# ScalarE issues the key loads in the middle of a group's second slot instead of at the end of its first

## The chip, the cores and the metric

The kernel runs on one core of one Trainium2 chip. The metric is the time of one execution on the device, in microseconds (us); lower is better. Engines are named as in the profile: PE is TensorE (PEld its weight loads), DVE is VectorE, ACT is ScalarE, POOL is GpSimd and SP is SyncE, which here only issues DMA transfers. A DMA instruction of SP or ACT is shown as SPq or ACTq: its duration is the time that the issuing queue spends on it, and its landing is when the data is there.

## The reference

Keys and values are one tensor, pooled 4 x 4 and projected; 4 batches of 12,288 tokens attend to 768 keys each, and every token then goes through a feed-forward layer of width 1,024 with a SoLU activation and a layer norm.

```python
kv_pool = kv.reshape(B, H // r, r, W // r, r, C).mean(axis=(2, 4))
k = v = kv_pool.reshape(B, -1, C) @ w_sr
s = scale * (q @ k.transpose(0, 2, 1))
a = np.exp(s - s.max(-1, keepdims=True))
x = (a / (a.sum(-1, keepdims=True) + 1e-09)) @ v
h = x @ w_in
e = np.exp(h - np.max(h, axis=-1, keepdims=True))
solu = h * (e / (np.sum(e, axis=-1, keepdims=True) + 1e-09))
ln = (solu - mean(solu)) / np.sqrt(var(solu) + 1e-06) * g_ln
out = ln @ w_out
```

## The kernel before

The 49,152 tokens are 384 tiles of 128 tokens. A **slot** is one step of the main loop, with a piece of work of several tiles at different stages; four slots make a **group** (512 tokens). The order of every instruction is written out by hand, so each engine's queue is that order with the other engines' instructions taken out. In slot `t` the kernel

- turns the scores of tile `t` into weights: `nm` (DVE, L611), the exponential `s` (ACT, L612), the high half of `phl` (ACT, L614), its low half (DVE, L622), and a DMA transpose of `phl` to `pT` (SP, L625);
- works on the hidden layer of tiles `t-11` and `t-10`: `u` (DVE, L741), the halves of `uhl` (POOL, L758 and L765), a DMA transpose of `uhl` to `uT` (SP, L780), the square `junk` of `u` for the variance (ACT, L806), the exponential `e` (ACT, L727);
- multiplies `uT` of tile `t-13` by the output weights (PE, L831; 24 weight loads and matmuls for a tile).

Once per group SP also loads the next queries (`qf`, 256 KB, L531), at the end of the group's last slot, and writes the finished rows (`out`, L863), and ACT scales the attended values to `xh` (L657), at the end of the first slot.

**Key loads.** While batch `b-1` is worked on, the 16 pieces of the next batch's keys come in as loads of 384 KB (`kv_load`, L230), which POOL adds up (`kv_add`, L241). `kv_plan` says in which slot each load and each add stands. The first 22 loads are issued by SP at the start; the other 42 are issued by ACT, one in every group or every second group. `kv_plan` rounds a piece's slot down to the first slot of its group, and the loop issues it as the last thing of that slot.

**Semaphores of transfers.** Each DMA instruction is given one of eight semaphores in turn (`DMAHW0` to `DMAHW7`), and does not start before the transfer that had this semaphore last has landed. Where a load stands in the program so decides on which earlier transfer it waits, and which later one waits on it.

Of the kernel before, what the change touches and what calls it, by code (L numbers as in the profile page):

```python
# [31 lines left out]
GT = 4  # L32
# [29 lines left out]
FIT_AT = 302  # L62

SOON = {0: (), 1: (8, 8), 2: (8, 8), 3: (27, 33), 4: (39, 45), 5: (51, 54)}
LATE = {6: (12, 16, 18), 7: (16, 20, 22)}


@with_exitstack
def kernel(
# [82 lines left out]
    def kv_alloc(b):  # L152
        for n, w, dt, bufs in (
            ("kT", NK, F32, 1),
            ("ksq", NK, BF16, 1),
            ("kss", 2, F32, 4),
            ("vf", NK, F32, 1),
        ):
            state[n, b] = bat.tile([P, w], dt, tag=n, name=f"{n}_{b}", bufs=bufs)
        for n, w in (("knm", 3), ("sv", 2), ("bb", 5), ("kq", 3), ("dg", P)):  # L160
            state[n, b] = (
                state[n, 0]
                if 0 < b < B
                else bat.tile([P, w], F32, tag=n, name=f"{n}_{b}", bufs=1)
            )
        for n, dt, bufs in (
            (("kwh", F32R, 1), ("kwl", F32R, 1))
            if b == 0 or b >= B
            else (("kh", F16, 2), ("kl", F16, 2))
        ):  # L170
            state[n, b] = bat.tile([P, NK], dt, tag=n, name=f"{n}_{b}", bufs=bufs)
        vhl = dmt.tile([P, 2 * NKC, P], F16, tag="vhl", name=f"vhl_{b}")
        state["vhl", b] = vhl
        state["vh", b], state["vl", b] = vhl[:, :NKC, :], vhl[:, NKC:, :]
# [327 lines left out]
    def kv_plan(b):  # L502


        for pos in range(RR):


            if b == 1 and pos in SOON:
                for half, slot in enumerate(SOON[pos]):
                    yield slot, [partial(kv_add, b, half, pos)]  # L510
                continue
            slot = 6 * pos - (28 if b == 1 else 30)
            load, *adds = (slot // GT * GT, slot + 3, slot + 5)
            if b == 1 and pos in LATE:
                load, *adds = LATE[pos]
            yield load, [partial(kv_load, b, pos)]
            if pos:
                for half, add in enumerate(adds):
                    yield add, [partial(kv_add, b, half, pos)]
        for slot, half, *fs in key_steps(b):  # L520
            yield slot, [partial(f, b, half) for f in fs]
# [18 lines left out]
    def wide(g):  # L540
        return g < GPB or g >= NG

    def q_scale(g):
        if wide(g) or NG <= g:
            return
        qf = state["qf", g // QL][:, (g % QL) * 512 : (g % QL + 1) * 512]
        nc.gpsimd.tensor_scalar(
            qf, qf, state["kq", g // GPB][:, 1:2], 1.0, op0=ALU.mult, op1=ALU.mult
        )
# [17 lines left out]
    def q_low(g):  # L567
        if NG <= g < NG + GPB:
            return
        qf = state["qf", g // QL][:, (g % QL) * 512 : (g % QL + 1) * 512]  # L570
        qh, ql = state["q", g]
        if wide(g):
            nc.gpsimd.tensor_tensor(
                in_tiles(ql), by_tile(qf), in_tiles(qh.bitcast(F32)), op=ALU.subtract
            )
        else:
            nc.gpsimd.tensor_tensor(ql, qf, qh, op=ALU.subtract)
# [52 lines left out]
    def values(g, qtr, part):  # L630
        share = {0: [0, 9, 9, 0], 1: [0, 6, 6, 6]}.get(
            g, [4, 5, 5, 4] if wide(g + 2) else [5, 5, 4, 4]
        )
        s0 = sum(share[:qtr])
        s1 = s0 + share[qtr]
        if s0 == s1:
            return
        cut = s0 + (s0 > 0 and (qtr > 1 or wide(g + 2)))
        s0, s1 = ((s0, cut), (cut, s1))[part]
        b = g * GT // TPB  # L640
        if s0 == 0 and s1:
            state["xa", g] = ps_x.tile([P, 512], F32, tag="x", name=f"xa_{g}")
        if s0 == s1:
            return
        xa, pT = state["xa", g], state["pT", g]
        vh, vl = state["vh", b], state["vl", b]
        seq = [(a, c, v) for c in range(NKC) for (a, v) in ((0, vh), (1, vh), (0, vl))]
        for n in range(s0, s1):
            a, c, v = seq[n]
            nc.tensor.matmul(  # L650
                xa, v[:, c, :], pT[:, :, a * NKC + c, :], start=n == 0, stop=n == len(seq) - 1
            )
# [386 lines left out]
    def key_steps(b):  # L1039
        steps = [  # L1040
            (70, 0, kv_kp, kv_ko), (71, 1, kv_kp, kv_ko), (74, 2, kv_kp, kv_ko),
            (72, 0, kv_sq), (75, 1, kv_sq),
            (77, 0, kv_kh), (79, 1, kv_kh),
            (78, 0, kv_kl), (80, 1, kv_kl),
        ]
        if b < B - 1:
            return steps + [
                (82, 0, kv_vp, kv_vo), (83, 1, kv_vp, kv_vo), (86, 2, kv_vp, kv_vo),
                (84, 0, kv_v_high), (85, 0, kv_v_low), (87, 1, kv_v_high), (88, 1, kv_v_low),
            ]  # L1050
        return steps + [
            (82, 0, kv_v_scale), (84, 1, kv_v_scale),
            (83, 0, kv_vt_high), (86, 1, kv_vt_high),
            (86, 0, kv_vt_low), (88, 1, kv_vt_low),
            (90, 0, kv_v_turn),
        ]
# [3 lines left out]
    def at(t, fn, *args):  # L1060
        if 0 <= t < NT:
            fn(t, *args)

    def at_last(t, fn, *args):

        if 0 <= t < NT and t % GT == GT - 1:
            fn(t // GT, *args)

    def at_soon(t, fn):

        at_last(t, fn) if t >= GT else fn(0) if t == GT - 2 else None

    plan = {}
    for b in range(1, B):
        for k, fs in kv_plan(b):
            plan.setdefault((b - 1) * TPB + k, []).append(fs)
# [4 lines left out]
    for slot in range(NT):  # L1081
        i = slot - LH
        av, qtr = divmod(slot - LAV - GT + 1, GT)
        tb, ti = divmod(slot, TPB)
        if ti == 12 and tb + 1 < B:
            kv_alloc(tb + 1)
        qs = GT if slot < 2 * GT else 2 * GT + 1 if slot < 3 * GT else 3 * GT + QSP
        todo = plan.pop(slot, [])
        at(slot, scores_exp)
        for f in held:  # L1090
            f()
        held = []
        if slot <= LH:
            at(slot - 1, scores_split)
        at(i - 1, hidden_u)
        at_last(slot - XSP - 1, values_split)
        if slot < 9:
            for f in fill.pop(slot, []):
                f()
        if 0 <= av < NG:  # L1100
            values(av, qtr, 0)
        if slot != 8:
            at(slot + 2 if slot < 8 else slot + 1, scores_pe)
        at_soon(slot - NORM, values_norm)
        at_last(slot - FSC, final_scale)
        at(i - 1, hidden_high)
        at(i - 1, hidden_low)
        at_last(slot - FSC, final_root)
        if slot < NT and 0 < qs < slot and (slot - 1 - qs) % GT == 0:
            q_low(slot // GT + 1)  # L1110
        if slot < NT and 0 < qs <= slot + 1 and (slot + 1 - qs) % GT == 0:
            q_scale((slot + 1) // GT + 1)
        if slot < NT - 1:
            at(i - 1, hidden_var)
        at(i, hidden_max)
        at(i, hidden_exp)
        if slot == NT - 1:
            hidden_var(i - 1)
        for f in fill.get(slot, []):
            f()  # L1120
        pairs = [st for st in todo if len(st) > 1 and st[0].func is not kv_add]
        for st in pairs:
            st[0]()
        if 0 <= av < NG:
            values(av, qtr, 1)
        for st in pairs:
            held += st[1:]
        if slot >= LH:
            at(slot, scores_split)
        at_soon(slot - NORM, values_recip)  # L1130
        at_soon(slot - NORM, values_recip_u)
        at(i + 1, hidden_pe)
        if slot < NT - 1:
            at(slot - LO, final_pe)
        at(i - 1, hidden_turn)
        if slot % GT == GT - 1:
            q_load(slot // GT + 3)
        at_last(slot - LO - 1, final_out)
        at_last(slot - XSP, values_out)
        for st in todo:  # L1140
            if st[0].func is kv_add:
                for f in st:
                    f()
            elif len(st) == 1:
                st[0]()
        if slot < NT and 0 < qs <= slot and (slot - qs) % GT == 0:
            q_split(slot // GT + 1)
# [182 lines left out]
```

## Time and profile before

| | before |
|---|---|
| time, median of 3 runs | 1836.55 us (1835.77 to 1844.36) |
| the profiled execution's own time | 1841.4 us |
| its span, first to last instruction | 1839.5 us |
| PE busy | 1818.2 us, 99% of the span |
| DVE, ACT, POOL busy | 1768.4, 1749.2, 1665.6 us (96%, 95%, 91%) |
| mean granted TensorE clock | 0.999 |
| key loads issued by ACT | 42 of 384 KB, 4.4 us to landing (median) |

A busy share is an average over the span. An engine that is busy for 99% of it leaves little for the others to win or lose by, so what counts here is the idle time of PE, and what ended it.

### The profile page before, as it was taken

What the parts mean: (1) busy time and instruction counts of PE and PEld (TensorE: products, weight loads), DVE (VectorE), ACT (ScalarE), POOL (GpSimd) and SP (SyncE); (2) the same over time, 40 slices, a digit from 0 to 9 for tenths busy, and PEclk for the clock granted to TensorE, in tenths of its full rate; (3) what the DMA queues carried; (4) which work ended last, traced back from release to release, by engine and by line L of the source; (5) the groups of instructions that cost most, each with busy time, mean ns of one, the idle gap of its engine ahead of it and who ended that gap; (6) DMA issues with size and microseconds to landing.
All of it is one profiled execution on the core that took longest, in us unless ns stands there. A gap on an engine that the chain in (4) does not pass through costs nothing.

```text
span 1839.5 us, 42799 instructions
## 1 busy us (share of the span) xinstructions
PE 1818.2 (99%) x15747; PEld 1216.9 (66%) x15747; DVE 1768.4 (96%) x2635; ACT 1749.2 (95%) x3129; POOL 1665.6 (91%) x1466
## 2 busy tenths in 40 slices
PE   8999999999999999999999999999999999999998
PEld 5577777777666666566666666666666666666666
DVE  6999999999999999999999999999999999999997
ACT  5999999999999999899999999999999999999997
POOL 5899999899999999889999999998988988888887
PEclk9999999999999999999999999999999999999999
DMA  8999999999999999999999999999999999999998
GB/s 301 202 243 241 237 242 242 237 230 231 250 230 250 250 233 234 225 245 235 235 244 249 236 243 248 244 233 221 233 240 231 222 230 229 235 227 236 223 226 170
DMA packets 1440026, 432.79 MB, mean 235 GB/s; under 512 B 1404608, under 2 KB 1408832, under 8 KB 1439552
## 3 DMA queue, kind: packets, MB, share of 16 engines
q1 hardware_dynamic: 1433616, 413.45, 111.3%
q10 hardware_dynamic: 6192, 16.52, 3.5%
q8 instruction: 126, 2.06, 0.5%
q14 instruction: 92, 0.75, 0.1%
HBM read 52.50 MB, written 25.17 MB: 42 GB/s over the span
## 4 chain that ended last, share of the span: by engine, by line
PE 82%; ACT 8%; DVE 3%; DMA 2%; issue 2%; POOL 2%; SPq 0%; DVEq 0%; POOLq 0%; ACTq 0%
PE o L831 24%; PE h L703 23%; PE s L590 18%; PE xa L650 17%; ACT e L727 2%; ACT junk L806 2%; ACT phl L614 2%; ACT s L612 1%; DMA uT<-uhl 1%; DMA kv<-in_kv_dram 1%; POOL uhl L765 1%; DVE junkd L711 1%; DVE nm L611 1%; POOL uhl L758 1%; DVE phl L622 1%
## 5 line engine op out<-in xcount | busy, mean ns | idle before, releaser
L765 POOL TENSOR_TENSOR uhl<-u,uhl 128x1024 f16<-128x1024 f32 x382 | 814.5, 2133 | 31.7
L831 PEld LDWEIGHTS <-uT 128*128 128x128 f16 x9072 | 537.2, 98 | 95.9 <-DMA uT<-uhl 9.6
L831 PE MATMUL o<-wch,uT 128*128 128x128 f16 x6048 | 568.2, 219 | 5.0 <-DMA uT<-uhl 4.8
L831 PE MATMUL o<-wcl,uT 128*128 128x128 f16 x3024 | 526.1, 219 | 0.0
L741 DVE SCALAR_TENSOR_TENSOR u<-h,rz,e 128x1024 f32<-128x1024 f32 x384 | 491.1, 1279 | 26.4 <-ACT e L727 18.9
L711 DVE TENSOR_SCALAR_CACHE_REDUCE junkd<-h,rz 128x1024 bf16<-128x1024 f32 x384 | 490.7, 1278 | 1.5 <-PE h L703 1.1
L758 POOL TENSOR_SCALAR uhl<-u 128x1024 f16<-128x1024 f32 x379 | 395.8, 1044 | 84.7 <-DVE u L741 76.4
L650 PE MATMUL xa<-pT,vhl 128*128 128x512 f16 x1728 | 469.8, 380 | 0.0
L727 ACT ACTIVATE e<-h,nm,rz 128x1024 f32<-128x1024 f32 x384 | 458.5, 1194 | 3.0 <-DVE junkd L711 3.0
L806 ACT ACTIVATE junk<-u,su 128x1024 bf16<-128x1024 f32 x384 | 438.0, 1141 | 0.1
L611 DVE TENSOR_REDUCE nm<-s 128x1 f32<-128x768 f32 x384 | 363.9, 948 | 16.8 <-PE s L590 13.1
L612 ACT ACTIVATE s<-s,nm 128x768 f32<-128x768 f32 x384 | 335.0, 872 | 41.1 <-DVE nm L611 40.9
L622 DVE SCALAR_TENSOR_TENSOR phl<-s,phl 128x768 f16<-128x768 f32 x384 | 365.6, 952 | 2.9 <-ACT phl L614 2.9
L614 ACT ACTIVATE phl<-s 128x768 f16<-128x768 f32 x384 | 311.1, 810 | 12.2
L703 PEld LDWEIGHTS <-xh 128*128 128x128 f16 x1536 | 141.0, 97 | 194.5 <-DVE phl L622 32.3
L650 PEld LDWEIGHTS <-vhl 128*128 128x128 f16 x1728 | 162.5, 98 | 135.5 <-issue 12.8
L703 PE MATMUL h<-w_in_h,xh 128*128 128x512 f16 x768 | 229.1, 380 | 1.6 <-DVE rz L685 1.0
L703 PE MATMUL h<-w_in_h,xl 128*128 128x512 f16 x768 | 228.5, 379 | 0.0
L703 PE MATMUL h<-w_in_l,xh 128*128 128x512 f16 x768 | 228.5, 379 | 0.0
L590 PEld LDWEIGHTS <-qh 128*128 128x128 f16 x1152 | 124.2, 113 | 43.7 <-issue 0.7
L590 PE MATMUL s<-kh,qh 128*128 128x384 f16 x576 | 140.6, 326 | 0.6 <-DVE u L741 0.6
L590 PE MATMUL s<-kh,ql 128*128 128x384 f16 x576 | 140.9, 326 | 0.0
(153 smaller groups left out, 1816.8 us busy)
## 6 DMA issues: line engine op xcount, KB each, us to landing
qf<-in_q_dram SPq DMA_DIRECT2D x96, 256.0 KB, 3.6
out_dram<-ob SPq DMA_DIRECT2D x96, 256.0 KB, 2.7
kv<-in_kv_dram ACTq DMA_DIRECT2D x42, 384.0 KB, 4.4
kv<-in_kv_dram SPq DMA_DIRECT2D x22, 384.0 KB, 7.5
pT<-phl SPq DMA_TRANSPOSE x384, 4.0
uT<-uhl SPq DMA_TRANSPOSE x378, 4.5
raw_in<-in_moe_w_in_dram SPq DMA_DIRECT2D x1, 1024.0 KB, 5.0
raw_out<-in_moe_w_out_dram SPq DMA_DIRECT2D x1, 1024.0 KB, 9.8
```

The costliest lines, as they stand in the source:

```text
L590: nc.tensor.matmul(s[:, half, :384], tokens(lh)[:, j, :], rh[:, half * 384 : (half + 1) * 384], start=n == 0, stop=n == 2,)
L611: nc.vector.tensor_reduce(nm, s, axis=AX.XY, op=ALU.max, negate=True)
L622: nc.vector.scalar_tensor_tensor(phl[:, 1], state.pop(("s", t)), SC, phl[:, 0], op0=ALU.mult, op1=ALU.subtract)
L650: nc.tensor.matmul(xa, v[:, c, :], pT[:, :, a * NKC + c, :], start=n == 0, stop=n == len(seq) - 1)
L703: nc.tensor.matmul(h[:, hs], lh[:, ts], rh[:, hs], start=n == 0, stop=n == 2)
L711: nc.vector.tensor_scalar(junk, state["h", t], state["rz", g][1][:, j : j + 1], None, op0=ALU.mult, op1=ALU.min, accum_out=nm,)
L727: nc.scalar.activation(e, state["h", t], AF.Exp, bias=nm, scale=state["rz", g][0][:, js], accum_out=state["z2", g][:, js],)
L741: nc.vector.scalar_tensor_tensor(u, state.pop(("h", t)), state["rz", g][2][:, j : j + 1], state.pop(("e", t)), op0=ALU.mult, op1=ALU.mult, ...
L758: nc.gpsimd.tensor_scalar(uhl[:, 0, :], u, 1.0, 1.0, op0=ALU.mult, op1=ALU.mult)
L765: low.tensor_tensor(uhl[:, 1, :], u, uhl[:, 0, :], op=ALU.subtract)
L806: nc.scalar.activation(junk, u, AF.Square, scale=-float(DFF), bias=su, accum_out=state["v3", g][:, j : j + 1],)
L831: nc.tensor.matmul(po[:, ts], uT[:, a * NFC + c, :], w[:, c, :], start=start, stop=stop)
```

## The change

Three edits. `kv_plan` puts a load one slot later: into the second slot of its group in place of the first (and the two hand-set entries of `LATE` with it). The loop issues the loads of a slot in its middle, ahead of the square (`hidden_var`), in place of at its end. And the loop's end passes the loads over, since they have been issued. The adds stay in their slots.

```diff
-LATE = {6: (12, 16, 18), 7: (16, 20, 22)}
+LATE = {6: (13, 16, 18), 7: (17, 20, 22)}
...
             slot = 6 * pos - (28 if b == 1 else 30)
-            load, *adds = (slot // GT * GT, slot + 3, slot + 5)
+            load, *adds = (slot // GT * GT + 1, slot + 3, slot + 5)
             if b == 1 and pos in LATE:
                 load, *adds = LATE[pos]
             yield load, [partial(kv_load, b, pos)]
...
             q_scale((slot + 1) // GT + 1)
+        for st in todo:
+            if st[0].func is kv_load:
+                st[0]()
         if slot < NT - 1:
             at(i - 1, hidden_var)
         at(i, hidden_max)
...
             if st[0].func is kv_add:
                 for f in st:
                     f()
-            elif len(st) == 1:
+            elif len(st) == 1 and st[0].func is not kv_load:
                 st[0]()
```

On ACT, at the load of piece 15 of the keys of batch 2 (slots 156 and 157), the order before is this; `xh` is the end of slot 156, `s` the start of slot 157.

```order
L727 ACTIVATE e_11135,z_36_10929<-h_11074,nm_146_11132,rz_10906 128x1024 [waits DVE_49]
L657 ACTIVATE xh_11176<-xa_10919,sv_115 128x512 [waits PE_49]
L230 DMA kv_15_11179<-in_kv_dram 128x768 [waits DMAHW6_49]
L612 ACTIVATE s_11119,z_all<-s_11119,nm_11181 128x2x384 [waits DVE_49]
L614 ACTIVATE phl_11184<-s_11119 128x768 [waits DMAHW0_49,Activation_49]
L806 ACTIVATE junk_11204,v_36_10930<-u_11186,su_11187 128x1024 [waits DVE_49]
```

And after the change, at the same place:

```order
L727 ACTIVATE e_11135,z_36_10929<-h_11074,nm_146_11132,rz_10906 128x1024 [waits DVE_49]
L657 ACTIVATE xh_11176<-xa_10919,sv_115 128x512 [waits PE_49]
L612 ACTIVATE s_11119,z_all<-s_11119,nm_11179 128x2x384 [waits DVE_49]
L614 ACTIVATE phl_11182<-s_11119 128x768 [waits DMAHW0_49,Activation_49]
L230 DMA kv_15_11202<-in_kv_dram 128x768 [waits DMAHW7_49]
L806 ACTIVATE junk_11204,v_36_10930<-u_11184,su_11185 128x1024 [waits DVE_49]
```

The load has moved behind two instructions, `s` and the high half of `phl`, and now waits for another semaphore.

On SP the sequence of transfers is the same before and after. What changes is the semaphore that a transfer gets and waits for. Before, at the same place (`qf` is the last transfer of slot 155, the first `pT` that of slot 156):

```order
L531 DMA qf_11107<-in_q_dram 128x512 [waits DMAHW4_49]
L625 DMA_TRANSPOSE pT_11140<-phl_11113 128x12x128 [waits DMAHW5_49,DVE_49,PE_49]
L780 DMA_TRANSPOSE uT_11174<-uhl_11126 128x16x128 [waits DMAHW7_49,Pool_49]
L625 DMA_TRANSPOSE pT_11140<-phl_11184 128x12x128 [waits DMAHW0_49,DVE_49]
L780 DMA_TRANSPOSE uT_11255<-uhl_11201 128x16x128 [waits DMAHW6_49,DMAHW1_49,Pool_49]
```

And after the change, down to the next group's queries:

```order
L531 DMA qf_11107<-in_q_dram 128x512 [waits DMAHW4_49]
L625 DMA_TRANSPOSE pT_11140<-phl_11113 128x12x128 [waits DMAHW5_49,DVE_49,PE_49]
L780 DMA_TRANSPOSE uT_11174<-uhl_11126 128x16x128 [waits DMAHW6_49,Pool_49]
L625 DMA_TRANSPOSE pT_11140<-phl_11182 128x12x128 [waits DMAHW0_49,DVE_49]
L780 DMA_TRANSPOSE uT_11255<-uhl_11199 128x16x128 [waits DMAHW1_49,Pool_49]
L863 DMA out_dram<-ob_11257 128x512 [waits DMAHW2_49,DVE_49]
L625 DMA_TRANSPOSE pT_11140<-phl_11266 128x12x128 [waits DMAHW3_49,DVE_49]
L780 DMA_TRANSPOSE uT_11327<-uhl_11278 128x16x128 [waits DMAHW4_49,PE_49,Pool_49]
L625 DMA_TRANSPOSE pT_11140<-phl_11332 128x12x128 [waits DMAHW5_49,DVE_49]
L780 DMA_TRANSPOSE uT_11396<-uhl_11348 128x16x128 [waits DMAHW6_49,PE_49,Pool_49]
L531 DMA qf_11398<-in_q_dram 128x512 [waits DMAHW7_49]
```

`DMAHW6` was the load's semaphore and `DMAHW7` that of the `uT` behind it; now they are the other way round. The load waits for the transfer that had `DMAHW7` before it, which in nearly all groups is a write of finished rows from the group before, and the next `qf`, ten transfers further on, waits for the load.

## Rows read from the trace of the kernel before

**Rows 1.** The page: busy time, share of the span and instructions of each engine.

```profile
PE 1818.2 (99%) x15747; PEld 1216.9 (66%) x15747; DVE 1768.4 (96%) x2635; ACT 1749.2 (95%) x3129; POOL 1665.6 (91%) x1466
```

**Rows 2.** The `uT` transposes of 75 to 1220 us; below, who waited (us, times).

```profile
L780 SPq DMA_TRANSPOSE uT<-uhl x245: 1334/2325/5451, 74.3 to 1215.9; - x123
...
  PEld L831: 9.6, 11
  PE o L831: 4.8, 5
```

**Rows 3.** The same of 1260 to 1780 us; nobody waited for these.

```profile
L780 SPq DMA_TRANSPOSE uT<-uhl x113: 1317/2027/4236, 1261.2 to 1778.5; - x113
```

**Rows 4.** The key loads of ACT: duration on the queue in ns (min/median/max), landing.

```profile
L230 ACTq DMA_DIRECT2D kv<-in_kv_dram x42: 334/335/362, 66.7 to 1190.0; - x42
...
DMA to landing us min/median/max: 3.6/4.4/7.8
```

**Rows 5.** SP's issues around two key loads: start, duration on the queue (us).

```profile
754.08 0.53 SPq L863 DMA_DIRECT2D out_dram<-ob  x1
...
759.77 1.70 SPq L780 DMA_TRANSPOSE uT<-uhl  x1
761.52 0.58 SPq L531 DMA_DIRECT2D qf<-in_q_dram  x1
762.21 4.23 SPq L625 DMA_TRANSPOSE pT<-phl  x1
...
214.26 1.75 SPq L780 DMA_TRANSPOSE uT<-uhl  x1
...
216.74 1.29 SPq L625 DMA_TRANSPOSE pT<-phl  x1
218.38 4.06 SPq L780 DMA_TRANSPOSE uT<-uhl  x1
```

**Rows 6.** ACT's instructions around these two loads and a third, in order of time.

```profile
760.70 0.34 ACTq L230 DMA_DIRECT2D kv<-in_kv_dram  x1
...
762.30 0.81 ACT L614 ACTIVATE phl<-s 128x768 f16<-128x768 f32 x1
763.00 1.14 ACT L806 ACTIVATE junk<-u,su 128x1024 bf16<-128x1024 f32 x1
...
216.54 0.33 ACTq L230 DMA_DIRECT2D kv<-in_kv_dram  x1
...
218.13 0.81 ACT L614 ACTIVATE phl<-s 128x768 f16<-128x768 f32 x1
...
703.22 0.33 ACTq L230 DMA_DIRECT2D kv<-in_kv_dram  x1
```

**Rows 7.** PE's first use of a `uT` behind these loads; in brackets PE's wait.

```profile
768.70 0.23 PE L831 MATMUL o<-wch,uT 128*128 128x128 f16 x1 [2.05 <-DMA uT<-uhl]
...
226.81 0.10 PEld L831 LDWEIGHTS <-uT 128*128 128x128 f16 x1
```

**Rows 8.** Single `uT` transposes: duration on the queue (ns), start, then landing (us).

```profile
L780 SPq DMA_TRANSPOSE uT<-uhl x1: 1698/1698/1698, 759.8 to 759.8; - x1
...
DMA to landing us min/median/max: 8.9/8.9/8.9
...
L780 SPq DMA_TRANSPOSE uT<-uhl x1: 1754/1754/1754, 214.3 to 214.3; - x1
...
DMA to landing us min/median/max: 3.8/3.8/3.8
...
L780 SPq DMA_TRANSPOSE uT<-uhl x1: 4058/4058/4058, 218.4 to 218.4; - x1
...
DMA to landing us min/median/max: 7.6/7.6/7.6
...
L780 SPq DMA_TRANSPOSE uT<-uhl x1: 4757/4757/4757, 702.3 to 702.3; - x1
...
DMA to landing us min/median/max: 6.7/6.7/6.7
```

## The prediction

> **What bounds the kernel now.** I read the page first: PE is busy for 1818.2 of 1839.5 us [rows 1]. The kernel is bound by PE, and a change that gives PE no less work can win only the idle time of PE that it takes away. So the second view is that of PE's waits. Beyond the first 75 us, in which the pipeline fills, one cause stands out: the output matmuls wait for the transposed activations `uT`, five times, 4.8 us together [rows 2]. The reader should see where these waits lie. All five, and all eleven of the weight loads, fall in the 1145 us in which key loads are issued; of the 113 transposes issued after the last key load none was late [rows 3]. The transposes and the key loads share the transfer engines, and the key loads make `uT` late. Nothing else of the 42 loads is seen on PE.
>
> The third view is the order of time around one such wait. A `uT` transpose was issued at 759.77, the key load at 760.70 and the queries at 761.52 [rows 5, 6]. The transpose then took 8.9 us to land [rows 8], and PE stood still for 2.05 us until it did [rows 7]. In a usual group the load comes later against the `uT` ahead of it: that one was issued at 214.26 and the load at 216.54, 2.28 us behind it [rows 5, 6], and it landed in 3.8 us [rows 8], untouched. There the load falls on the next one, issued at 218.38: 7.6 us to landing [rows 8], so at 225.98, and PE loaded its first piece at 226.81 [rows 7], with 0.83 us to spare and no wait. So in a usual group the load costs spare time alone; it costs PE time where it is issued less than a microsecond behind a `uT`.
>
> **The change part by part.** What is moved is one ACT instruction in each of 42 places, with its transfer of 384 KB. Nothing is added to or taken from any engine's work.
>
> *When it is issued.* The load now stands behind the exponential and the high half of `phl`. In the two groups `phl` started at 762.30 and 218.13, where the loads had started at 760.70 and 216.54 [rows 6]. A load is taken up as the instruction ahead of it starts, as it was at 760.70, so it moves by 1.60 and 1.59 us: call it 1.6.
>
> *ACT's time.* The load takes 334 to 362 ns on ACT's queue [rows 4]. It now lies beside `phl`, which runs for 0.81 us, and the square behind it started 0.70 us after `phl` did [rows 6]: 0.34 us are covered, cost 0. With that cover gone it would be 42 x 0.34 = 14 us of ACT, whose idle share is 5% of the span [rows 1].
>
> *The wait that comes with the new place.* The load waits for a write of finished rows. In the example the last one was issued at 754.08 [rows 5], 8.2 us ahead of the new place; even with the landing of the slowest load, which has more bytes (7.8 us [rows 4]), it would be down before that. Behind the load stand the square and the exponential `e`, for which DVE's `u` waits. I take 0. The next `qf` waits for the load to land; it comes two and a half slots later, some 12 us at 1839.5 / 384 = 4.8 us a slot, and loads land in 3.6 to 7.8 us [rows 4]: 0. POOL's first add comes two to four slots after the new place, at least 9 us: 0 again, if the load isn't slower than any so far.
>
> *The wait that goes.* In the group of the 2.05 us the load falls 0.93 us behind its `uT` now, and will fall 0.93 + 1.6 = 2.5 us behind it. That is the distance of the usual group (2.28 us), where the transpose landed in 3.8 us [rows 8] instead of 8.9. It would land 5 us earlier, against a wait of 2.05: the wait goes, and I take the other four to go the same way. Gain: 4.8 us of the profiled execution's 1841.4.
>
> *What is late next.* In a usual group the load is now issued at 218.13, beside the `uT` of 218.38 instead of 1.84 us ahead of it. No row shows a `uT` issued within half a microsecond of a load. The rows on either side bound it. Issued 0.90 us ahead of a load (702.32 against 703.22) it landed in 6.7 us, 0.93 us ahead in 8.9; issued 1.84 us behind one, in 7.6 [rows 5, 6, 8]. PE needs it 226.81 - 218.38 = 8.43 us after its issue [rows 7]. At 6.7 us there are 1.7 us to spare, at 8.9 PE waits for 0.47 us in each group: 42 x 0.47 = 20 us. I take 7.6, the row at the other side of the gap and nearest in what stands ahead in SP's queue (the same `qf` and `pT`): the transfer engines have the same bytes to move before this `uT` is through, whether the load goes ahead of the `pT` or beside it. So no wait, cost 0, and a bound of 20 us.
>
> The Trainium skill, "DMA: Bandwidth & Descriptors", section "Queues, rings and completion order", says that a transfer's semaphore is raised by a strongly ordered write, which lands only after every earlier write of that transfer engine, across its queues. By that rule a transpose in flight beside a load lands no sooner than the load's earlier writes. By the rows for the load (4.4 us median, 7.8 at most) that would be 222.5 to 225.9 in the usual group, still ahead of 226.81, so the sum would stay as it is.
>
> *The sum.* 1841.4 - 4.8 = 1836.6 us for the profiled execution. That is the median of the runs shown (1836.55; the profiled one is 4.9 us above it), so I read the median run as one that has hardly any of these waits. The change then takes the waits from executions like the profiled one, and leaves the median where it is. I say 1836.5.
>
> **The rivals.** A difference under 0.5% (9.2 us) is about what a measurement of this kernel can't tell from no change.
>
> *The next `uT` is late instead* (slower). The mechanism is the bound above: the load's bytes now run beside `pT` and the second `uT`. It decides from 8.43 - 7.6 = 0.83 us of extra delay in the usual group; at 1.05 us extra it is 0.22 us in each of 42 groups, the 9.2 us of the measure. For it: the slowest transposes of the trace are those that share the transfer engines with a load from early on [rows 8]. Against it: the same rows at 6.7 and 7.6, and that the work ahead isn't more. Beyond 0.5%: 1846 to 1856 us, chance 0.06. Part of it, some groups late by a few tenths, 1838 to 1845 us: 0.14.
>
> *The load's issue holds up ACT* (slower). SP's queue is busy with a `pT` or a `uT` for 1.3 to 4.2 us around the new places [rows 5]. Were ACT's issue to wait until SP's was over, the square and all behind it would come later by up to the median 2.3 us [rows 2] less the 0.5 that `phl` still covers: 42 x 1.8 = 76 us, 1912 at most. Against it: the load of 703.22 took 0.33 us [rows 6] inside an SP issue that began at 702.32 and lasted 4.76 us [rows 8]. Chance 0.02.
>
> The Trainium skill, "Perfetto Trace Analysis", section "DMA Instruction — HWDGE (DVE, Sync)", has a rule that speaks for this: the generator of descriptors is locked for exclusive use while one sequencer's transfer is being set up, and the others' wait is in the profiled duration. The row at 703.22 doesn't show such a wait.
>
> *It does nothing to the waits*, since where a load falls against a `uT` drifts by more than 1.6 us: the median stays and the spread too, 1836.6 to 1841.4 us: 0.08.
>
> *The runs shown hold waits as well*, and have 4.8 us to give: 1836.55 - 4.8 = 1831.8 us. Against it: two of three runs lie within 0.8 us of each other, which waits that come by chance wouldn't give. 0.05, and 0.01 for more than 0.5% faster, for which PE's busy time leaves no source.
>
> **How the numbers follow.** The forecast has 0.64, its own range 1835 to 1838 us. The range of 8 in 10 runs from 1833.5 (between the floor of the runs and the last rival) to 1843.0 (the middle of the partly late groups, 42 x 0.15 us above the forecast); outside lie 0.06 below, and above 0.06, 0.02 and a third of the 0.14. Faster by over 0.5% 0.01, within 0.91, slower 0.08 (0.06 + 0.02).
>
> **What would show it.** In the changed kernel's profile the loads start with `phl` (L614) and still take 0.34 us; the square has no idle time ahead of it. The `uT` issued ahead of a load lands in about 4 us everywhere; the one beside it in 7 to 8. PE's waits for `uT` are near 0, and PE's idle time beyond 75 us under 2 us. I am wrong if PE's waits for `uT` are of tens of short ones at the second `uT`, if a load's duration on ACT grows beyond 0.5 us, or if `qf` is late behind a load.

## The result, and the profile after

The changed kernel takes 1864.12 us (median of 6 runs, 1857.79 to 1875.31), the kernel before 1840.75 us in the runs beside it (6 runs, 1835.77 to 1844.36). The ratio is 1.0119, with a 95% interval of 1.0083 to 1.0156: the change made the kernel slower by 1.2%. (Ratios, here and below, are formed from undisturbed runs alone, so they need not be the quotient of the medians.) The forecast of 1836.5 us and its range up to 1843.0 are both missed.

The profiled execution took 1860.2 us, 18.8 more than that of before, and its span is 18.9 us longer (1858.4 against 1839.5). On the page, PE's busy time answers to [rows 1]:

```profile
PE 1821.9 (98%) x15747; PEld 1216.7 (65%) x15747; DVE 1770.0 (95%) x2635; ACT 1751.5 (94%) x3129; POOL 1664.9 (90%) x1466
```

It grew by 3.7 us for the same instructions. The rest is waiting. These are the `uT` transposes of 75 to 1220 us and who waited for them, as in [rows 2], with their time to landing (min/median/max):

```profile
L780 SPq DMA_TRANSPOSE uT<-uhl x242: 1596/2287/8652, 69.9 to 1217.3; - x121
...
  PEld L831: 35.5, 35
  PE o L831: 19.8, 23
...
DMA to landing us min/median/max: 3.8/4.9/10.6
```

PE's output matmuls wait 23 times in place of 5, and 19.8 us in place of 4.8: 15.0 us more. With the 3.7 of busy time that is 18.7 of the 18.9 us. Behind the last key load nothing has changed; for the transposes of 1260 to 1780 us nobody waited, as in [rows 3]:

```profile
L780 SPq DMA_TRANSPOSE uT<-uhl x114: 1317/2141/4257, 1257.1 to 1778.1; - x114
...
DMA to landing us min/median/max: 3.6/4.2/7.1
```

The loads themselves, as in [rows 4], are as cheap on ACT's queue as they were, but the slowest lands in 10.5 us in place of 7.8:

```profile
L230 ACTq DMA_DIRECT2D kv<-in_kv_dram x42: 334/335/362, 68.3 to 1209.5; - x42
...
DMA to landing us min/median/max: 3.6/4.8/10.5
```

Two groups show how it goes wrong. From the order of time: SP, ACT and PE around the load of 246.58, and the same around that of 1003.27 (start, duration; in brackets PE's wait), to be read beside [rows 5 to 7]:

```profile
246.03 1.43 SPq L625 DMA_TRANSPOSE pT<-phl  x1
247.55 7.89 SPq L780 DMA_TRANSPOSE uT<-uhl  x1
...
246.57 0.81 ACT L614 ACTIVATE phl<-s 128x768 f16<-128x768 f32 x1
246.58 0.36 ACTq L230 DMA_DIRECT2D kv<-in_kv_dram  x1
247.28 1.14 ACT L806 ACTIVATE junk<-u,su 128x1024 bf16<-128x1024 f32 x1
...
258.16 0.23 PE L831 MATMUL o<-wch,uT 128*128 128x128 f16 x1 [2.54 <-DMA uT<-uhl]
...
1003.87 1.41 SPq L625 DMA_TRANSPOSE pT<-phl  x1
1005.38 3.89 SPq L780 DMA_TRANSPOSE uT<-uhl  x1
...
1003.27 0.34 ACTq L230 DMA_DIRECT2D kv<-in_kv_dram  x1
...
1013.80 0.23 PE L831 MATMUL o<-wch,uT 128*128 128x128 f16 x1 [1.48 <-DMA uT<-uhl]
```

The load starts with `phl`, and the square stands 0.70 us behind it: ACT pays nothing. In both groups the `uT` that PE waits for is the one issued behind the load. The time to landing of the first load and its `uT`, then of the second and its own:

```profile
L230 ACTq DMA_DIRECT2D kv<-in_kv_dram x1: 362/362/362, 246.6 to 246.6; - x1
...
DMA to landing us min/median/max: 9.1/9.1/9.1
L780 SPq DMA_TRANSPOSE uT<-uhl x1: 7890/7890/7890, 247.6 to 247.6; - x1
...
DMA to landing us min/median/max: 10.6/10.6/10.6
...
L230 ACTq DMA_DIRECT2D kv<-in_kv_dram x1: 340/340/340, 1003.3 to 1003.3; - x1
...
DMA to landing us min/median/max: 4.4/4.4/4.4
L780 SPq DMA_TRANSPOSE uT<-uhl x1: 3888/3888/3888, 1005.4 to 1005.4; - x1
...
DMA to landing us min/median/max: 8.4/8.4/8.4
```

At 1003.27 the load landed in its usual time, and the `uT` in a time like those of [rows 8]; PE needed it 1013.80 - 1.48 - 1005.38 = 6.94 us after its issue, though, not 8.43 us as in the group that the prediction took. I call this a **plain** delay. At 246.58 the load itself was slow. The DMA view shows the difference: packets, bytes and queues (q10 is ACT's, q1 is SP's), first of 1005.0 to 1006.5, then of 249 to 254 us:

```profile
DMA packets 100, 0.30 MB, mean 200 GB/s; under 512 B 1, under 2 KB 1, under 8 KB 100
...
q10 hardware_dynamic: 96, 0.29, 78.8%
q1 hardware_dynamic: 4, 0.01, 1.4%
...
DMA packets 618, 0.34 MB, mean 69 GB/s; under 512 B 551, under 2 KB 551, under 8 KB 618
...
q1 hardware_dynamic: 544, 0.14, 72.5%
q10 hardware_dynamic: 74, 0.21, 39.0%
```

In the plain group the load has the transfer engines to itself while the transposes stand still (4 packets), at 200 GB/s. In the other both queues move at once and both crawl: 69 GB/s together for five microseconds. I call that a **crawl**.

### The profile page after: what moved, and what is told of

The parts are those of the page before. It is cut to its first block, busy times and chain, and to the rows that moved or that the text cites. A ratio compares the mean times of both kernels' runs of the same rounds, so it can differ in the third digit from the quotient of the medians.

```text
span 1858.4 us, 42798 instructions
## 1 busy us (share of the span) xinstructions
PE 1821.9 (98%) x15747; PEld 1216.7 (65%) x15747; DVE 1770.0 (95%) x2635; ACT 1751.5 (94%) x3129; POOL 1664.9 (90%) x1466
## 4 chain that ended last, share of the span: by engine, by line
PE 62%; ACT 9%; DMA 9%; POOL 8%; DVE 6%; issue 5%; SPq 0%; POOLq 0%; DVEq 0%
PE o L831 19%; PE h L703 17%; PE s L590 13%; PE xa L650 13%; DMA uT<-uhl 8%; POOL uhl L765 3%; ACT junk L806 2%; ACT e L727 2%; POOL uhl L758 2%; ACT phl L614 2%; DVE nm L611 2%; ACT s L612 2%; DVE junkd L711 1%; DVE phl L622 1%; DMA kv<-in_kv_dram 1%
## 5 line engine op out<-in xcount | busy, mean ns | idle before, releaser
L831 PE MATMUL o<-wch,uT 128*128 128x128 f16 x6048 | 568.9, 219 | 20.1 <-DMA uT<-uhl 19.8
L650 PEld LDWEIGHTS <-vhl 128*128 128x128 f16 x1728 | 162.8, 98 | 135.6 <-issue 12.9
```

Source lines behind the costliest of these rows:

```text
L650: nc.tensor.matmul(xa, v[:, c, :], pT[:, :, a * NKC + c, :], start=n == 0, stop=n == len(seq) - 1)
L831: nc.tensor.matmul(po[:, ts], uT[:, a * NFC + c, :], w[:, c, :], start=start, stop=stop)
```

## The experiments

The theory tested (A in the expectations): while a load's bytes are in flight, a `uT` beside them lands late, and moving the load 1.6 us later took that much from the spare time of that `uT`, the time between its landing and PE's need of it. The rivals are that ACT's order or the semaphores are at fault, that the place beside `qf` is, that each load costs a fixed time, and that the second queue is what matters. All ratios are to the kernel before, in runs on the same chip.

**Few bytes at the changed place.** Against the changed kernel:

```diff
-        eng.dma_start(
-            t, kv[b - 1, r, :, two * NK : (two + 1) * NK].rearrange("p (h k) -> p h k", h=2)
-        )
+        src = kv[b - 1, r, :, two * NK : (two + 1) * NK].rearrange("p (h k) -> p h k", h=2)
+        few = eng is nc.scalar
+        eng.dma_start(t[:, :, :48], src[:, :, :48]) if few else eng.dma_start(t, src)
...
```

> The changed place, but each of the 42 loads of ScalarE brings only the first 48 of its 384 columns per half (48 KB in place of 384); the adds repeat these columns, so the keys of batches 2 to 4 are not the reference's. Instruction order, semaphores and the work of every engine are those of the changed kernel. Theory A (the load's bytes run beside the uT transpose issued within about 2.5 us behind it, which then lands after 7 to 10 us and PE waits): with an eighth of the bytes the waits for uT nearly go, 1836 to 1839 us, uT waits of PE under 3 us. Theory B (the place on ScalarE's queue, ahead of the square, or the changed semaphores cost the time): as the changed kernel, 1858 to 1870 us.

1835.68 us (1835.15 to 1836.11, 10 runs), ratio 0.9951 (0.9927 to 0.9976). Of all `uT` of 75 to 1230 us none is listed as waited for:

```profile
L786 SPq DMA_TRANSPOSE uT<-uhl x249: 1315/2199/3954, 73.9 to 1226.8; - x125
...
DMA to landing us min/median/max: 3.6/4.4/6.7
```

Instructions, order and semaphores are those of the changed kernel, and POOL, whose adds read the 48 columns repeatedly, is busy for 1665.7 us against 1664.9; only the bytes are gone, and with them the whole loss. So ACT's order and the semaphores are cleared. I take this time as the floor of the loop, since no `uT` is late any more: the median of the kernel before on that chip, 1843.08, lies 7.4 us above it.

**Half of the bytes, as one transfer.** The same edit with 192 columns in place of 48.

> The changed kernel with half of the bytes: each load brings 192 of the 384 columns of each half, 192 KB as one transfer at the changed place (POOL adds the 192 columns twice over, at the same cost, so the keys are wrong and the output is not the reference's). With 48 KB the time was 1835.7 us, with 384 KB 1864.1. Theory A (the load's time on the transfer engines is added to that of the uT beside it, and PE waits for what exceeds the spare time): a uT lands 1.5 to 2 us sooner than in the changed kernel, under 7 us where it was 7 to 8.5, so of the stalls only those of the few slowest uT stay: 1836 to 1842 us. Rival S (the number of loads and not their size, above some small size): 1855 to 1866 us.

1836.92 us (1836.02 to 1840.21, 10 runs), ratio 0.9954 (0.9934 to 0.9973). PE's waits for `uT`, and the landing of `uT`:

```profile
  PE o L837: 1.1, 2
...
DMA to landing us min/median/max: 3.6/4.7/8.1
```

As A expected: against 48, 192 and 384 KB a load stand 1835.7, 1836.9 and 1864 us, or ratios of 0.995, 0.995 and 1.012. The `uT` issued from 0.5 us ahead of a load to 4.6 us behind it land in 4.9, 5.4 and 7.3 us (medians). The landing grows with the bytes, while the cost in time is not in proportion to them; that the spare time is the threshold is A's reading of this.

**Three other places for the whole load**, on ACT as before (the two entries of `LATE` move with it each time). The end of the second slot, from the kernel before:

```diff
...
-            load, *adds = (slot // GT * GT, slot + 3, slot + 5)
+            load, *adds = (slot // GT * GT + 1, slot + 3, slot + 5)
```

> The loads at the end of the group's second slot, one slot (4.6 us) behind the place of before, the same distance from the uT transposes but without the query load beside them. Theory A: the uT behind the load is issued 1.8 to 3.8 us after it as before, and there are 256 KB less in front of it, so it lands sooner than the 7.4 us of before: PE's waits for uT under 5 us, 1836 to 1840 us, not slower than before. Theory B (place ahead of the square costs, the end of a slot doesn't): as before, 1836 to 1844. If lateness itself (the adds, the next qf waiting for the load) were the cause: slower than the changed kernel, over 1860.

1862.32 us (1857.55 to 1869.77, 4 runs), ratio 1.0103 (1.0046 to 1.0159). The end of the last slot of the group before (`- 1` in place of `+ 1`):

> The loads at the end of the last slot of the group before, one slot ahead of the place of before, ahead of the query load by some 4 us. Theory A: the uT behind the load is 1.8 to 3.8 us after it as before, without the query load in front: PE's waits for uT under 5 us, 1836 to 1840 us. The query load then comes beside the next uT, as it does in groups without a key load, where no uT is late. Theory B: as before, 1836 to 1844.

1862.30 us (1852.24 to 1873.28, 7 runs), ratio 1.0090 (1.0053 to 1.0126). The middle of the third slot (the changed kernel with `+ 2`):

> The loads in the middle of the third slot, ahead of the square as in the changed kernel, one slot later. Theory A: the distance to the uT behind it is that of the changed kernel (0.3 to 2.4 us), but the query load (256 KB) is out of the way, so uT lands in 6 to 7.5 us against a window of 7 to 8.5: some waits, 2 to 10 us, 1838 to 1848 us, clearly under the changed kernel. Theory B: as the changed kernel, 1858 to 1870, since the place on ScalarE's queue is the same.

1851.79 us (1849.30 to 1857.57, 10 runs), ratio 1.0037 (1.0008 to 1.0066). No place that I tried away from `qf` was better than the old one, so the loss doesn't need `qf` beside the load. My numbers for all three fell: 1836 to 1840 us for the first two, 1838 to 1848 for the last, of which only "clearly under the changed kernel" held. The first lies where I had put lateness as such (over 1860), but the middle of the third slot is later still and loses less, and with 48 KB a load as late as the changed kernel's costs nothing. What the trace of the end of the second slot shows is again loads close to a `uT`: nine were issued 0.5 to 1.3 us behind one, that `uT` took up to 11.2 us, and these nine hold 12.9 of its 15.1 us of waits.

**Between `s` and `phl`**, earlier in the second slot. Against the changed kernel, in the part that turns scores into weights:

```diff
...
         nc.scalar.activation(s, s, AF.Exp, bias=nm, accum_out=state["z", g][:, j : j + 1])
+        for st in plan.pop(("load", t), []):
+            st[0]()
...
-        for st in todo:
-            if st[0].func is kv_load:
-                st[0]()
```

> The whole load between the exponential s and the high half of phl, about 1 us ahead of the changed place and 0.6 us behind the place of before. Theory A (what counts is where the load falls against the second uT of its group): the uT comes about 1 us later against the load than in the changed kernel, so the groups in which it came 1.5 to 2.4 us behind now have it 2.5 to 3.4 us behind, where it lands sooner, and the groups in which it came within 0.9 us behind now come into the bad distance, with 1 us more room: 1843 to 1858 us, between the two kernels. Rival B (the second slot as such is bad, for the semaphores or for ACT's order): as the changed kernel, 1860 to 1866 us.

1859.20 us (1846.19 to 1860.94, 10 runs), ratio 1.0068 (1.0039 to 1.0098). It lies a microsecond outside both expectations. Its profiled execution happens to be the fastest of the ten, so where the other nine lost their time isn't in a trace; this run decides nothing.

**The load in halves, in two slots.** Against the changed kernel:

```diff
...
+        eng.dma_start(t[:, 0, :], src[:, 0, :])
+        state["rest"] = partial(eng.dma_start, t[:, 1, :], src[:, 1, :])
...
+        if "rest" in state:
+            state.pop("rest")()
         for st in todo:
             if st[0].func is kv_load:
                 st[0]()
```

> The load of the changed kernel cut into its two halves of 192 KB: the first at the changed place, the second at the same place of the third slot. Theory A (the time that the load's bytes spend on the transfer engines beside a uT transpose is what makes that uT late): each half holds a uT up by half as much, 1.5 to 2 us less than a whole load, which is more than most of the stalls of the changed kernel (0.3 to 1.5 us each); so PE waits less than half as long for uT, under 8 us, and the time is 1837 to 1846 us. Rival S (each load costs a fixed time by its being there, whatever its bytes): twice as many loads, so the time is 1864 us or more.

1845.60 us (1844.21 to 1848.97, 10 runs), ratio 1.0010 (0.9983 to 1.0037), PE's waits 7.9 us. Twice the loads with the same bytes cost less than half of the waits, as A expected (under 8 us, 1837 to 1846); a fixed cost of each load, whatever its bytes, is out.

**SP in place of ACT**, which leaves one queue. Behind the queries, at the end of the last slot of the group before:

```diff
...
-            load, *adds = (slot // GT * GT, slot + 3, slot + 5)
+            load, *adds = (slot // GT * GT - 1, slot + 3, slot + 5)
...
-            yield load, [partial(kv_load, b, pos)]
+            yield load, [partial(kv_load, b, pos, nc.sync)]
```

> SP issues the load, right behind the queries at the end of the last slot of the group before; all large transfers are then in one queue. Theory A (bytes on the transfer engines, whichever queue they come from): the transposes behind the load in the queue land up to 4 us later, the first pT and uT above all; PE waits as long as in the kernel with ACT's load at that place (1862 us) or longer, 1855 to 1880 us. Rival Q (only a load from a second queue breaks into a transpose that is under way; one that waits its turn in the same queue does not): the uT ahead of the load is untouched, the one behind has the time of two transposes to spare, and the time is 1836 to 1842 us.

1849.21 us (1844.50 to 1853.36, 10 runs), ratio 1.0008 (0.9978 to 1.0037), against 1862.30 and 1.0090 for ACT's load at that place. And at the end of the first slot, where SP's load stands between the first slot's `uT` and the second slot's `pT` (only the second edit):

> SP issues the load at the end of the first slot, right behind that slot's uT. Theory A (bytes, whichever queue): the load runs beside or ahead of the second pT and uT, and the second uT, with 6.6 to 8.6 us to be there, is late in about half of the groups as in the changed kernel: 1850 to 1870 us. Rival Q (only a second queue breaks into a transpose under way): the uT ahead is untouched, and the one behind starts with the load half done: 1836 to 1843 us.

1849.48 us (1843.90 to 1855.08, 10 runs), ratio 1.0020 (0.9993 to 1.0047). The loads of this kernel and PE's waits for `uT`:

```profile
L230 SPq DMA_DIRECT2D kv<-in_kv_dram x41: 572/572/1465, 92.2 to 1205.7; - x41
...
DMA to landing us min/median/max: 3.8/4.2/6.2
...
PE o L831 <- DMA uT<-uhl: 11.5, 14, 1.5
```

Both expectations missed: each time lies between A and the rival. The trace tells why. The slowest load lands in 6.2 us and the longest wait is 1.5 us, where the changed kernel has 10.5 and 3.3. One queue does away with nearly all of the crawl and leaves the plain delay. That is no gain everywhere: at this place ACT's load is the kernel before itself, with 4.8 us of waits against SP's 11.5.

**The changed kernel once more**, unedited.

> The changed kernel once more, unedited, on the chip of the two kernels beside it, as their measure. Both theories: slower than the kernel before by 0.8 to 1.6%, and the waits for uT lie in other groups than in its first profile, since they follow from where a group's uT happens to fall against the load. If the waits lay in the same groups, the place of each would be set by the program and not by drift.

1876.08 us (1861.46 to 1898.80, 4 runs), ratio 1.0118 (1.0069 to 1.0167), as expected. Its profiled execution took 1878.57 us, and loads and waits tell more of the crawl:

```profile
L230 ACTq DMA_DIRECT2D kv<-in_kv_dram x42: 334/334/398, 68.2 to 1228.9; - x42
...
DMA to landing us min/median/max: 3.6/5.0/11.0
...
PE o L831 <- DMA uT<-uhl: 33.2, 24, 4.9
```

The slow loads are not those of the first profile: there the first two to land late were issued at 68.31 and 111.24, here at 180.57 and 219.60. So the program alone doesn't set which group crawls; drift between the engines would do it, but that is argued and not shown.

**Quarters in four slots**, on ACT. As the halves, but with four pieces of 96 KB and

```diff
...
+        if state.get("rest"):
+            state["rest"].pop(0)()
```

> All bytes, but each load in quarters of 96 KB, one at the changed place of each of four slots. Theory A: a quarter holds a uT up by 0.8 to 1 us, which fits into the spare time of nearly all uT; PE's waits for uT are under 3 us and the time 1836 to 1841 us, faster than both kernels. Rival P (the load's total of bytes is what counts, wherever it is spread, since every uT then is late by a little and in half of the groups the spare time is short): as the kernel with halves, 1843 to 1850 us.

1841.49 us (1838.41 to 1843.76, 12 runs) against 1845.21 (1835.86 to 1856.84, 23 runs) for the kernel before: ratio 0.9974 (0.9952 to 0.9997). Faster than the kernel before, by a quarter of a per cent (the interval ends just short of no change), clearly faster than the changed one, and steadier than both. The time lies half a microsecond above A's range and under the rival's; spreading all the bytes still leaves 3.4 us of waits and some 6 us to the floor:

```profile
PE o L837 <- DMA uT<-uhl: 3.4, 7, 0.9
```

**Quarters issued by SP**, each ahead of the slot's `pT`.

```diff
...
-            yield load, [partial(kv_load, b, pos)]
+            yield load, [partial(kv_load, b, pos, nc.sync)]
...
```

> Quarters of 96 KB again, one in each of four slots, but issued by SP, each ahead of the slot's pT, so that no second queue is left. Two parts of the loss have shown themselves: a plain one (the load's bytes ahead of a uT, waits of 0.1 to 1.5 us where spare time is short) and one of two queues (loads that take 5.5 to 11 us to land while the transpose beside them crawls, waits of 1 to 5 us; SP's whole loads had next to none of these). Theory A2 (both parts are real and quarters cure the first, one queue the second): no quarter takes over 5.5 us, PE's waits for uT are no more than with ACT's quarters (3.4 us), and the time is 1836 to 1841 us. Rival Q2 (SP's queue being in order, each quarter now delays the pT and uT behind it in every slot): 1842 to 1850 us, slower than ACT's quarters at 1841.5.

1868.99 us (1866.25 to 1870.31, 6 runs), ratio 1.0123 (1.0078 to 1.0167): my expectation failed outright, the rival had the direction right and the size too small. Waits of PE, and the landing of `uT`:

```profile
PE o L837 <- DMA uT<-uhl: 19.2, 32, 1.5
...
POOL ka L247 <- DMA kv<-in_kv_dram: 8.7, 11, 1.6
PE xa L656 <- DMA pT<-phl: 6.6, 7, 1.8
...
DMA to landing us min/median/max: 3.7/4.2/6.5
```

No `uT` is slow here, and no quarter takes over 4.9 us to land. PE now waits for the `pT` behind the quarter as well (6.6 us). The `uT` are quick but issued late: between the issue of a `uT` and PE's need of it lie 5.5 us (median of 75 to 1230 us), against 6.8 with ACT's quarters. What makes them late no run takes apart. It may be that the `pT` held back holds back the whole chain down to `uhl`; but POOL, which makes `uhl`, now also waits for quarters, 8.7 us in 11 waits, where on ACT it waited for none.

**Plain delay and crawl in all profiles.** Each load was put with PE's waits of over 50 ns at the output matmuls, from 2 us ahead of its issue to 16 behind it. A load, or piece of one, that took over 5.5 us to land counts as slow; the split into crawl (waits beside slow loads) and plain delay (the rest) goes by this measure.

| kernel | median us | PE's wait for `uT`, 75 to 1820 us | slow loads | waits beside these |
|---|---|---|---|---|
| before | 1840.75 | 4.8 | 4 of 42 | 4.8 |
| changed | 1864.12 | 19.8 | 11 | 9.2 |
| changed, second profile | 1876.08 | 33.2 | 15 | 26.1 |
| ACT, end of second slot | 1862.32 | 15.1 | 13 | 14.5 |
| ACT, end of slot before | 1862.30 | 12.8 | 7 | 9.7 |
| ACT, middle of third slot | 1851.79 | 11.5 | 7 | 3.3 |
| SP, end of slot before | 1849.21 | 9.6 | 3 | 0.0 |
| SP, end of first slot | 1849.48 | 11.5 | 2 | 0.8 |
| ACT, between `s` and `phl` | 1859.20 | 6.8 | 6 | 3.3 |
| 192 KB, ACT | 1836.92 | 1.1 | 3 | 0.0 |
| 48 KB, ACT | 1835.68 | 0.0 | 0 | 0.0 |
| halves, ACT | 1845.60 | 7.9 | 6 of 84 | 0.9 |
| quarters, ACT | 1841.49 | 3.4 | 1 of 168 | 0.0 |
| quarters, SP | 1868.99 | 19.2 | 0 of 167 | 0.0 |

With whole loads on ACT the crawl makes 3 to 26 us of waits; on SP, under one. The plain delay makes 0 to 11 us on ACT and about 10 on SP. Not tried: a `uT` issued earlier against PE's need, which would take the spare time out of the question.

## Why the prediction was wrong

**Right.** The 1.6 us of the move, the cost of 0 on ACT, the 0 for the load's wait and for `qf` and the adds: the square follows `phl` with no idle time, a load takes 334 to 362 ns as before, and with 48 KB the same program has none of the loss. The rival that a load's issue holds up ACT fell with these.

**The step that failed is "What is late next".** It took 0, with a bound of 20 us, and PE waited 15.7 us for the `uT` of the table below, in 15 groups of 40; the rival "The next `uT` is late instead" is what happened, beyond its heavy case (1846 to 1856 us), to which I gave 0.06. Three things were wrong in it.

First, it measured the landing of the second `uT` from that `uT`'s own issue (7.6 us) and kept this when the load moved. By its own rows the `uT` landed at 225.98, which is 9.44 us behind the *load's* issue, and PE needed it at 226.81, 10.27 behind it. If a late landing follows the load, a move of 1.6 us leaves 8.67 us, and that `uT` is 0.77 us late. Over all groups, for the `uT` issued from 0.5 us ahead of a load to 4.6 us behind it:

```
                                  before       changed
uT counted                        38           40
issued behind the load, median    2.4 us       1.6 us
landed behind the load, median    9.1          8.5
                        range     7.3 to 10.7  6.0 to 12.2
needed by PE, median              10.5         8.9
landed more than 9.0 behind it    20           18
PE waited (over 50 ns)            0            15
```

PE's need moved against the load by the full 1.6 us; the landing moved by 0.6, since part of the `uT` now start sooner behind a load. The 20 landings over 9.0 us in the trace of before were there to be read: with PE's need 1.6 us sooner and the landings left where they were, 21 of the 38 would be late, by 10.4 us in all. That is an estimate from these rows, without the loads that became slow.

Second, one usual group stood for all 42. The `uT` of 218.38, 0.25 us behind the moved load, would have 8.43 us from its issue until PE needs it. In the changed kernel 21 of the 40 were issued 1.0 to 3.0 us behind the load and had 7.1 us (median); 13 of these were waited for, against 1 of the 16 that came closer.

Third, the crawl. The transpose of 8.9 us in [rows 8] belongs to a group whose load was slow as well (7.8 us, the slowest of [rows 4]); the one of 6.7 us, at the same distance, had a load of 3.9 us. I read the two as a matter of distance to the `uT` ahead. "The wait that goes" went in part: the `uT` issued 0.5 to 1.3 us ahead of a load (six before, four in the changed kernel) cost PE 4.2 us before and 1.5 now. But the new place made 11 slow loads in place of 4. The sum also left PE's busy time where it was, and it grew by the 3.7 us above. What starts a crawl in one group and not in the next, I can't say: distance alone doesn't sort them.

**The reading of the median** failed too. I took the run of 1836.55 us for one with hardly any waits, and 0.9 us above the floor it will have been one, though it has no trace; but further runs put the median of before at 1840.75 to 1845.91, with single ones from 1835.77 to 1864.03. Three runs were too few for that. The rival that the runs shown hold 4.8 us of waits fell as well: the floor is 1835.7, not 1831.8.

The Trainium skill, "DMA: Bandwidth & Descriptors", section "Queues, rings and completion order", says that a transfer engine takes turns between the queues that have work, packet by packet. Were the turns even, the two queues would move about as many packets each while both have work. The rows show 96 packets of the load to 4 of the transposes in the plain group, and 74 to 544 at a third of the rate in the crawl. Whether the profile's packets are those of the page, and whether the transposes had work queued in the plain group, no run here shows. The rates themselves price the two, as estimates: a load of 0.39 MB at 200 GB/s keeps a `uT` waiting for 2 us; the crawl moved 0.34 MB in 5 us, which would have taken 1.7 at 200 GB/s.

## What to carry to other kernels

When a transfer is moved, measure what lands behind it from the issue of the transfer that is moved, and set that against when it is needed, over all groups and not in a usual one: the tail of that list is the bound. A transfer off the critical path is not free because it has time to land; it takes spare time from whatever shares the transfer engines, and cutting it into pieces that each fit into this spare time (96 KB here) did more than any place tried for the whole. The choice of the queue cuts both ways: on SP's own queue nearly all of the crawl was gone, but pieces ahead of every `pT` cost more than they saved.

## What the runs showed of the hardware

A copy from DRAM on ACT's queue and transposes on SP's can fall to 69 GB/s together, where the load alone went at 200, and transposes right behind the crawl of 246.58 at 293 (windows of PE in the changed kernel: stretch; us and PE busy; granted clock; DMA share; GB/s):

```profile
251.00:252.00 1.00, 1.00 (x22) 1.00 0.06 10
252.00:253.00 1.00, 1.00 (x10) 1.00 0.83 56
...
256.00:257.00 1.00, 0.00 (x0) 1.00 1.29 293
```

A long wait of PE can cost twice. In the second profile of the changed kernel PE stood still for 4.94 us until 887.25; the same windows around it:

```profile
884.00:886.00 2.00, 0.00 (x0) 0.76 1.65 234
886.00:888.00 2.00, 0.76 (x8) 0.50 0.73 159
...
890.00:892.00 2.00, 2.00 (x7) 0.53 1.13 266
892.00:894.00 2.00, 2.00 (x12) 1.00 1.21 275
```

The clock fell from 2.4 to 1.2 GHz in the wait and stayed there for some 5 us after PE had work again, half of which is lost. PE's busy time in that execution is 1827.4 us, 9.2 more than before. In five of its stretches of 20 us the granted clock is below 1.00 (0.83 to 0.99), all in or right behind waits of 2.7 to 4.9 us; there a wait costs more than its length. Not every such wait does this: behind one of 2.85 us, at 231, the clock stayed at 1.00. A clock of 0.98 from 100 to 200 us is part of the 3.7 us of the first profile too.
